# Chunk attention, soft MoE and maxout on one core: q and k repacked by token row, fp32 transposes, another order of steps and 20 ring buffers

## The chip, the cores and the metric

The kernel runs on one core of a Trainium2 chip. The metric is the device time of one execution in microseconds. Engine names are those of the profile: PE is TensorE's matmuls and PEld its weight loads, DVE is VectorE, ACT is ScalarE, POOL is GpSimd, SP is SyncE, which issues nearly all DMAs. Each engine works through its own instructions in order.

## What is computed

```python
# attention inside chunks of 64 tokens; q, k, v: 8 x 8 heads x 576 x 64
scores = scale * q_c @ k_c.T
attn = exp(scores - max(scores)); attn /= sum(attn) + 1e-9
x = (attn @ v_c) as 4608 tokens x 512
# soft MoE: 8 experts with 4 slots each, F = 1024
logits = x @ phi
d = softmax over the tokens (axis 0) of logits
slot_input = d.T @ x
slot_out[e] = maximum(slot_input[e] @ w1[e], 0) @ w2[e]
c = softmax over the slots (axis 1) of logits
x = c @ slot_out
# maxout, d_ff = 768
h = maximum(maximum(x @ m_w1, x @ m_w2), x @ m_w3)
out = h @ m_wo
```

The inputs q, k, v and phi, w1, w2 are fp32; the four maxout weights arrive as 64-bit floats, whose high and low words the kernel decodes to fp32 itself ("raw" weights below).

## The kernel before

**Loop over items.** A unit is 256 tokens; an item is half of the heads of a unit, so there are NI = 36 items. The loop at L580 walks the letters of ORDER (L63) once for each item i and calls for each its step from STEPS (L565); a step works on an item before or after i, by its offset. The order of the letters is the order of the instructions on every engine's queue, and so also of the DMA issues on SP's.

The steps that matter here: "LQ", "LK" load tile j = i + 5 of q and k (load_T: two heads of 512 tokens, 256 KB, two buffers each in raw_p); "LS" loads the last tokens of all heads in steps 1 to 4 (load_S); "LV" loads v of item i + 2 (three tiles); "LR" loads a piece of raw maxout weights (load_raw, L488); "LC" and "LD" load a quarter of an expert weight chunk (load_quarter). "VS" makes shifted copies of v on POOL (L207 to L210). "Tq", "Tk" transpose q and k on PE (emit_T), "qe", "ke" copy the result from PSUM to SBUF on ACT (emit_evac, L252). "S" makes the scores (L271), "mx" and "sub" take off the maximum on DVE, "PT" transposes the result and "PTe" takes the exponential on ACT, "PV" multiplies by v (L319), "rd", "rec", "nrm" divide by the sum on DVE, "XT" and "XTe" transpose x and copy it. Every fourth step the group steps follow: "lg" logits, "lc", "st", "ex" statistics and exponential, "eT", "eTe" its transpose, "sm", "sa" slot matmul and its sum. "df" (POOL), "da" (ACT) and "d0" (DVE) decode raw weights.

**Transposes of q and k.** emit_T reads the loaded tile as bf16 halves: for each head e of two, each token row r of four and each half h, one transpose of 128x64 by a bf16 identity, 16 for a tile; the evacuation interleaves the halves again. The tiles of "Tq", "Tk", "PT", "XT", "lg", "eT" and "sm" take turns in one PSUM pool of four tiles (ps_t). The scores have a tile of their own (ps_s), of which the columns 256 to 511 in each of two banks are unused.

**Ring buffers.** Expert weights come in 32 chunks of 1 MB. Twelve buffers are there from the start; as pools of the loop are released, open_rings adds single ones, NSLOT = 7 in all, each with its load. The expert phase begins behind the loop and a tail that finishes the last items, the last group and the slot softmax (L601 to L643). For each of eight experts emit_w1, emit_ht and emit_w2 run, and each expert's end asks for four more chunks. With expert 5 (of 0 to 7) the three loads of the output weights (load_wo) and the tiles of the combine weights take ring buffers.

**Output.** TAIL orders the entry to the maxout stage by hand; then h_mm and out_mm (L892, L929) run over blocks of 512 tokens to the end.

## Time and profile before

| what | value |
|---|---|
| median of 3 runs | 447.15 us (439.87 to 447.57) |
| the profiled execution's own time | 438.74 us |
| its span, first to last instruction | 436.9 us |
| PE busy | 401.2 us, 92% |
| DVE, ACT, POOL busy | 239.1, 214.8, 168.8 us |
| HBM read, written | 74.51 MB, 9.44 MB |

The profile is of one execution. Busy time is the time in which an engine runs instructions; matmuls overlap in the pipeline, so a merged row of matmuls can be longer than what it adds to the chain. "A <- B" is a wait of A that B's end released. The DMA share is the mean busy share of 16 DMA engines, and since transfers overlap it can pass 1. The span falls into the loop (to about 171 us), the tail of the loop and the slot softmax, the experts (from about 187 us) and the output stage (from about 241 us).

### The profile page before, as it was taken

How to read it: one execution, taken by the hardware profiler on the slowest of the kernel's cores; microseconds unless marked ns; L12 is line 12 of the kernel's file. 1: busy time of each engine (PE TensorE's matmuls, PEld its weight loads, DVE VectorE, ACT ScalarE, POOL GpSimd, SP SyncE). 2: the span in 40 equal slices, each digit the busy share in tenths (PEclk: the TensorE clock that was granted, in tenths of full speed). 3: DMA queues.
4: the chain of work that ended last, by engine and by line, in shares of the span. 5: the costliest groups of instructions: out<-in, count | busy, mean ns of one | idle time of the engine just before them, and what ended most of it. 6: DMA issues, size and time to landing. Idle time of an engine off the chain costs nothing.

```text
span 436.9 us, 13243 instructions
## 1 busy us (share of the span) xinstructions
PE 401.2 (92%) x5519; PEld 301.2 (69%) x5519; DVE 239.1 (55%) x515; ACT 214.8 (49%) x393; POOL 168.8 (39%) x291
## 2 busy tenths in 40 slices
...
PEclk9999998999999999999999799999999999999999
...
DMA packets 65275, 84.80 MB, mean 194 GB/s; under 512 B 4800, under 2 KB 42688, under 8 KB 65216
## 3 DMA queue, kind: packets, MB, share of 16 engines
...
q8 instruction: 43, 0.70, 0.7%
...
HBM read 74.51 MB, written 9.44 MB: 192 GB/s over the span
## 4 chain that ended last, share of the span: by engine, by line
PE 75%; DMA 10%; DVE 5%; ACT 4%; issue 3%; POOL 1%; SPq 1%; ACTq 0%; POOLq 0%; DVEq 0%
PE ops L929 35%; PE h L892 9%; PE pso L319 4%; DMA vt<-in_v_dram 4%; PE psqr L239 3%; PE pskr L239 3%; PE pst L354 3%; PE pss L271 3%; DMA qr<-in_q_dram 3%; PE pst L303 3%; DMA kr<-in_k_dram 2%; PE hps L706 2%; PE so L737 2%; PE slp L428 2%; PE lg L372 2%
## 5 line engine op out<-in xcount | busy, mean ns | idle before, releaser
L929 PE MATMUL ops<-wo,hhi 128*128 128x512 f32 x432 | 137.3, 399 | 0.0
L908 POOL TENSOR_TENSOR hlo<-a,hhi 128x512 fp32r<-128x512 f32 (+1 forms) x60 | 71.4, 1193 | 109.2 <-ACT hhi L905 109.2
L929 PEld LDWEIGHTS ops<-wo,hhi 128*128 128x128 f32 x432 | 81.3, 190 | 18.6
L929 PE MATMUL ops<-wo,hlo 128*128 128x512 f32 x216 | 86.0, 398 | 0.0
L901 DVE TENSOR_TENSOR a<-h,a 128x512 f32<-128x512 f32 (+1 forms) x60 | 38.2, 637 | 87.0 <-ACT a L897 86.1
L897 ACT COPY a<-h 128x512 f32<-128x512 f32 (+1 forms) x60 | 32.7, 546 | 97.1 <-PE h L892 97.0
L929 PEld LDWEIGHTS ops<-wo,hlo 128*128 128x128 f32 x216 | 41.2, 191 | 10.2
L252 ACT COPY qT<-psqr 128x1024 uint16<-128x1024 uint16 x36 | 36.7, 1020 | 19.0 <-PE pss L271 15.9
L902 DVE TENSOR_TENSOR a<-h,a 128x512 f32<-128x512 f32 (+1 forms) x60 | 38.3, 639 | 6.5 <-DVE a L901 0.5
L207 POOL COPY vt<-vt 128x256 f32<-128x256 f32 x36 | 14.6, 405 | 64.1 <-DMA vt<-in_v_dram 57.2
L905 ACT CAST hhi<-a 128x512 fp32r<-128x512 f32 (+1 forms) x60 | 34.6, 581 | 9.4 <-DVE a L902 9.4
L252 ACT COPY kT<-pskr 128x1024 uint16<-128x1024 uint16 x36 | 36.3, 1008 | 0.5 <-PE pskr L239 0.5
L287 DVE TENSOR_REDUCE mx<-pss 128x8 f32<-128x512 f32 x36 | 24.8, 688 | 20.8 <-PE pss L271 20.2
L892 PE MATMUL h<-cstt,ast 128*128 128x512 f32 (+1 forms) x120 | 32.6, 384 | 0.4 <-DVE a L902 0.3
L239 PE MATMUL psqr<-identb,qr 128*64 128x128 bf16 x512 | 22.5, 233 | 10.2 <-DMA qr<-in_q_dram 6.4
L209 POOL COPY vt<-vt 32x256 f32<-32x256 f32 x72 | 29.5, 410 | 4.3
L210 POOL COPY vt<-vt 32x256 f32<-32x256 f32 x72 | 28.9, 401 | 4.4
L359 ACT COPY xT<-pst 128x512 f32<-128x512 f32 x36 | 21.4, 593 | 17.8 <-PE lg L372 12.4
L319 PE MATMUL pso<-vt,pT 64*64 64x66 f32 x1152 | 27.1, 227 | 3.0 <-issue 2.1
L239 PE MATMUL pskr<-identb,kr 128*64 128x128 bf16 x512 | 22.1, 231 | 7.6 <-issue 3.6
L308 ACT ACTIVATE pT<-pst 128x512 f32<-128x512 f32 x36 | 21.5, 596 | 14.6 <-PE pst L303 14.5
L319 PEld LDWEIGHTS pso<-vt,pT 64*64 64x64 f32 x1152 | 21.6, 136 | 9.9 <-issue 7.8
...
## 6 DMA issues: line engine op xcount, KB each, us to landing
...
w<-in_moe_w_dram SPq DMA_DIRECT2D x44, 256.0 KB, 5.4
qr<-in_q_dram SPq DMA_DIRECT2D x32, 256.0 KB, 5.4
kr<-in_k_dram SPq DMA_DIRECT2D x32, 256.0 KB, 5.0
out_dram<-ob SPq DMA_DIRECT2D x32, 256.0 KB, 2.0
vt<-in_v_dram SPq DMA_DIRECT2D x30, 256.0 KB, 4.9
r<-in_moe_w_dram SPq DMA_DIRECT2D x18, 256.0 KB, 5.2
...
```

The source lines that it names most:

```text
L209: nc.gpsimd.tensor_copy(out=t[p:p + 32, :, 130:194], in_=t[p + 32:p + 64, :, 64:128])
L210: nc.gpsimd.tensor_copy(out=t[p + 32:p + 64, :, 64:128], in_=t[p:p + 32, :, 0:64])
L239: nc.tensor.transpose(dst, src[:, e, r, h, :], identb, tile_position=(0, 64 * e))
L252: copier(eng, j)(out=o, in_=x)
L319: nc.tensor.matmul(ps[64 * cp:64 * cp + 64, c2, 66 * h:66 * h + 66], lhsT=t[64 * c2:64 * c2 + 64, h, 64 * cp:64 * cp + 64], rhs=vt[i % NV] ...
L892: nc.tensor.matmul(p, lhsT=a_st[t][:, i, f0:f0 + 128], rhs=cst(t0, n), start=True, stop=True)
L897: nc.scalar.copy(out=h_a[b, f], in_=h_ps[b, f][0])
L901: nc.vector.tensor_tensor(out=a, in0=ps[1], in1=a, op=ALU.max)
L902: nc.vector.tensor_tensor(out=a, in0=ps[2], in1=a, op=ALU.max)
L905: nc.scalar.copy(out=h_t[b][0][:, f, :], in_=h_a[b, f])
L908: nc.gpsimd.tensor_tensor(out=h_t[b][1][:, f, :], in0=h_a.pop((b, f)), in1=h_t[b][0][:, f, :].bitcast(F32), op=ALU.subtract)
L929: nc.tensor.matmul(ps, lhsT=a[:, f, 128 * t:128 * t + 128], rhs=wo_h[f // 2][:, f % 2, w, :], start=(f == 0 and n == 0), stop=(f == FB - 1 ...
```

## The change

- A step of its own ("Rq", "Rk", emit_R) copies each loaded q or k tile into a pair tile with the token row r outermost, then head and width; q's copy runs on ACT, k's on POOL. The pair tiles have one buffer each.
- emit_T makes four fp32 transposes of 128x128 out of each pair tile, one per row r, and writes the columns into PSUM in the order in which they are used: 16 bytes apart for q, 8 bytes apart in two orders for k. The evacuation is a plain copy of 128x512 fp32.
- Transposes are emitted for tile i + 2 and not i + 3; the copy is that of tile i + 3. Probability transposes and their exponential move to the item's own step.
- Logits and the transpose of the exponential use the free columns of the scores' PSUM tile (spare).
- ORDER has the steps in another order: on SP "LD LV LR LQ LS LK LC" for "LR LC LQ LS LV LD LK"; on PE "S Tq PV sm lg eT Tk XT PT" for "S PT Tq sm eT XT PV lg Tk".
- raw-weight buffers go from three to two; NSLOT goes from 7 to 8. One ring opens at item NI - 4, one at NI - 3, and one at the start of the expert phase. To make room, the experts' hidden tiles lie in acc, which is cleared once it has been used, and the stacks of the combine weights lie in ring buffers, which are taken in another order.
- The bf16 identity goes. Other edits only rewrite views.

```diff
--- before
+++ after
@@ -61,10 +61,10 @@
         "H3 C2 X1 M2 H4 Y0 C3 o5 X2 Y1 C4 M3 H5 s1 Y2 C5 X3 Y3 M4 X4 M5 Y4 X5 Y5 s0"
     )
     ORDER = (
-        "LR qe ex S LC PT Tq LQ sm PTe mx sub sa ss da eT ke XT LS df PV LV d0 XTe "
-        "rd rec lg eTe VS LD Tk LK lc st nrm"
+        "df S LD Tq PV mx qe sm sub rd da lg eT sa LV VS Rq eTe Tk rec ke ex XT PT PTe LR "
+        "nrm lc Rk LQ LS XTe d0 LK LC st ss"
     )
-    NSLOT = 7
+    NSLOT = 8
     DUS = (0, 1, 8, 2, 3, 4, 5, 6, 7)
     J8 = 4 * DUS.index(8)
     STK = (5, 1, 2)
@@ -72,7 +72,6 @@
 
     const = ctx.enter_context(tc.tile_pool(name="const", bufs=1, side="left"))
     ident = const.tile([128, 128], F32, name="ident")
-    identb = const.tile([128, 128], BF16, name="identb")
     phi_sb = const.tile([128, KM, NS], F32, name="phi_sb")
     lsb = const.tile([128, NG, 128], F32, name="lsb")
     acc = const.tile([128, DM], F32, name="acc")
@@ -147,8 +146,9 @@
     w1_p = tc.alloc_tile_pool(name="w1p", bufs=1, side="right")
     v_p = tc.alloc_tile_pool(name="vp", bufs=1, side="right")
     q_p = tc.alloc_tile_pool(name="qp", bufs=3, side="right")
+    pair_p = tc.alloc_tile_pool(name="pair", bufs=1, side="right")
     raw_p = tc.alloc_tile_pool(name="raw", bufs=2, side="right")
-    r64_p = tc.alloc_tile_pool(name="r64", bufs=3, side="right")
+    r64_p = tc.alloc_tile_pool(name="r64", bufs=2, side="right")
     ps_t = p1.enter_context(tc.tile_pool(name="ps_t", bufs=4, space=PSUM))
     ps_q = ps_t
     ps_s = p1.enter_context(tc.tile_pool(name="ps_s", bufs=1, space=PSUM))
@@ -156,6 +156,7 @@
 
     NV = 3
     KENG, QENG, XENG = "AAAA", "AAAA", "AAAA"
+    PENG = {"qr": "A", "kr": "P"}
 
     def copier(eng, i):
         return nc.scalar.copy if eng[i % 4] == "A" else nc.vector.tensor_copy
@@ -214,42 +215,43 @@
     def last_unit(j):
         return J8 <= j < J8 + 4
 
+    pair = {}
+
+    def emit_R(j, nm):
+        if last_unit(j):
+            src = special[nm][:, 2 * (j - J8):2 * (j - J8) + 2]
+            if j == J8 + 3:
+                special.pop(nm)
+        else:
+            src = raw.pop((nm, j))
+        t = pair_p.tile([128, 4, 2, D], F32, tag=nm, name="p" + nm)
+        o = t.rearrange("p r m d -> p m r d")
+        if PENG[nm] == "A":
+            nc.scalar.copy(out=o, in_=src)
+        else:
+            (nc.vector if PENG[nm] == "D" else nc.gpsimd).tensor_copy(out=o, in_=src)
+        pair[nm, j] = t
+
     def emit_T(j, nms=("qr", "kr")):
         for nm in nms:
-            if last_unit(j):
-                src = special[nm][:, 2 * (j - J8):2 * (j - J8) + 2]
-                if j == J8 + 3:
-                    special.pop(nm)
-            else:
-                src = raw.pop((nm, j))
-            src = src.bitcast(BF16).rearrange("p m r (d h) -> p m r h d", h=2)
-            ps = ps_q.tile([128, 2, 512], BF16, tag="t", name="ps" + nm)
-            for h in range(2):
-                for r in range(4):
-                    for e in range(2):
-                        pe = ps[64 * e:64 * e + 64, h]
-                        if nm == "qr":
-                            dst = pe[:, 128 * r:128 * r + 128]
-                        else:
-                            dst = pe[:, 256 * (r // 2):256 * (r // 2) + 256]
-                            if last_unit(j):
-                                dst = dst[:, 128 * (1 - r % 2):128 * (1 - r % 2) + 128]
-                            else:
-                                dst = dst.rearrange("p (c s j) -> p c s j", s=2, j=16)[:, :, 1 - r % 2]
-                        nc.tensor.transpose(dst, src[:, e, r, h, :], identb, tile_position=(0, 64 * e))
+            src = pair.pop((nm, j))
+            ps = ps_q.tile([128, 2 * UNIT], F32, tag="t", name="ps" + nm)
+            for r in range(4):
+                if nm == "qr":
+                    if last_unit(j):
+                        o = ps.rearrange("p (c i r) -> p r i c", c=B, r=4)[:, r]
+                    else:
+                        o = ps.rearrange("p (i r) -> p r i", r=4)[:, r]
+                elif last_unit(j):
+                    o = ps.rearrange("p (c s i r) -> p s r i c", c=B, s=2, r=2)[:, 1 - r % 2, r // 2]
+                else:
+                    o = ps.rearrange("p (c s j r) -> p s r c j", s=2, j=16, r=2)[:, 1 - r % 2, r // 2]
+                nc.tensor.transpose(o, src[:, r].rearrange("p m d -> p (m d)"), ident)
             tq[nm, j] = ps
 
     def emit_evac(j, nm, eng, to):
         t = q_p.tile([128, 2 * UNIT], F32, tag=nm, name=nm)
-        n = 4 if nm[0] == "q" else 2
-        o, x = t.bitcast(U16), tq.pop((nm[0] + "r", j)).bitcast(U16)
-        if last_unit(j):
-            o = o.rearrange("p (c i r h) -> p c i r h", c=B, r=n, h=2)
-            x = x.rearrange("p h (r i c) -> p c i r h", r=n, c=B)
-        else:
-            o = o.rearrange("p (i r h) -> p i r h", r=n, h=2)
-            x = x.rearrange("p h (r i) -> p i r h", r=n)
-        copier(eng, j)(out=o, in_=x)
+        copier(eng, j)(out=t, in_=tq.pop((nm[0] + "r", j)))
         to[j] = t
 
     def emit_qevac(i):
@@ -259,6 +261,7 @@
         emit_evac(i, "kT", KENG, kT)
 
     s_ps = {}
+    spare = [None]
 
     def emit_S(i):
         ps = ps_s.tile([128, 2, 512], F32, tag="s", name="pss")
@@ -278,6 +281,7 @@
             for j in (j0, j0 + 1):
                 qT.pop(j)
                 kT.pop(j)
+        spare[0] = ps[:, :, 256:384]
         s_ps[i] = ps[:, :, 0:4 * CH].rearrange("p e (g k) -> p e g k", g=4)
 
     mxs = {}
@@ -365,8 +369,8 @@
 
     lgs = {}
 
-    def emit_logits(g):
-        lgs[g] = ps_t.tile([128, 128], F32, tag="t", name="lg")
+    def emit_logits(g, ps=None):
+        lgs[g] = ps if ps is not None else ps_t.tile([128, 128], F32, tag="t", name="lg")
         for kk in range(KM):
             for t in range(4):
                 nc.tensor.matmul(
@@ -409,8 +413,9 @@
 
     eps = {}
 
-    def emit_eT(g):
-        ps = ps_t.tile([128, 128], F32, tag="t", name="eps")
+    def emit_eT(g, ps=None):
+        if ps is None:
+            ps = ps_t.tile([128, 128], F32, tag="t", name="eps")
         nc.tensor.transpose(ps, e_sb[g], ident)
         eps[g] = ps
 
...
@@ -515,7 +519,6 @@
     sched.enter_context(tc.manual_schedule())
     if True:
         make_identity(nc, ident)
-        nc.vector.tensor_copy(out=identb, in_=ident)
         for j in range(2):
             load_T(j, "qr")
             load_T(j, "kr")
@@ -527,12 +530,15 @@
         load_raw(0)
         nc.sync.dma_start(out=phi_sb, in_=phi.rearrange("(k p) s -> p k s", p=128))
         for j in range(3):
-            emit_T(j)
-            if j < 2:
-                emit_qevac(j)
-                emit_kevac(j)
+            emit_R(j, "qr")
+            emit_R(j, "kr")
             load_T(j + 2, "qr")
             load_T(j + 2, "kr")
+            if j == 2:
+                break
+            emit_T(j)
+            emit_qevac(j)
+            emit_kevac(j)
         load_raw(1)
         nc.gpsimd.memset(ones1, 1.0)
 
@@ -565,16 +571,17 @@
         STEPS = {
             "LR": lambda i: load_raw(i + 1) if 0 < i < len(dec) - 1 else None,
             "LQ": item(lambda j: load_T(j, "qr"), 5), "LK": item(lambda j: load_T(j, "kr"), 5),
+            "Rq": item(lambda j: emit_R(j, "qr"), 3), "Rk": item(lambda j: emit_R(j, "kr"), 3),
             "LV": item(load_v, 2), "LC": lstep_c, "LD": lambda i: lstep_c(i) if i % 2 else None,
             "LS": lambda i: load_S(i - 1) if 1 <= i <= 4 else None,
             "VS": item(emit_vswap, 0),
-            "qe": item(emit_qevac, 2), "S": item(emit_S, 0), "PT": item(emit_PT, -1), "PTe": item(emit_PTe, -1),
+            "qe": item(emit_qevac, 2), "S": item(emit_S, 0), "PT": item(emit_PT, 0), "PTe": item(emit_PTe, 0),
             "da": dstep("a"), "df": dstep("f"), "ke": item(emit_kevac, 2), "ex": group(emit_exps, 7), "sm": group(emit_slot_mm, 9),
-            "sa": group(emit_slot_acc, 9), "Tq": item(lambda i: emit_T(i, ("qr",)), 3), "mx": item(emit_max, 0),
+            "sa": group(emit_slot_acc, 9), "Tq": item(lambda i: emit_T(i, ("qr",)), 2), "mx": item(emit_max, 0),
             "sub": item(emit_sub, 0), "XT": item(emit_XT, -2), "XTe": item(emit_XTe, -2),
             "d0": dstep("m"), "PV": item(emit_PV, -1), "rd": item(emit_rd, -1),
-            "rec": item(emit_rec, -1), "nrm": item(emit_norm, -1), "eT": group(emit_eT, 8), "eTe": group(emit_eTe, 8),
-            "Tk": item(lambda i: emit_T(i, ("kr",)), 3), "lg": group(emit_logits, 6), "lc": group(emit_lcopy, 6),
+            "rec": item(emit_rec, -1), "nrm": item(emit_norm, -1), "eT": group(lambda g: emit_eT(g, spare[0][:, 1]), 8), "eTe": group(emit_eTe, 8),
+            "Tk": item(lambda i: emit_T(i, ("kr",)), 2), "lg": group(lambda g: emit_logits(g, spare[0][:, 0]), 6), "lc": group(emit_lcopy, 6),
             "st": group(emit_stats, 6), "ss": group(emit_ssum, 7),
         }
         for i in range(NI):
@@ -582,13 +589,15 @@
                 STEPS[name](i)
             if i == len(dec) + 1:
                 r64_p.release()
-                open_rings(1)
                 nc.vector.tensor_reduce(
                     out=sel, in_=ident.rearrange("p (g s) -> p s g", g=4), axis=AX.X, op=ALU.max
                 )
             if i == NI - 4:
                 raw_p.release()
                 open_rings(1)
+            if i == NI - 3:
+                pair_p.release()
+                open_rings(1)
         q_p.release()
         open_rings(1)
 
@@ -599,8 +608,6 @@
                 nc.tensor.transpose(warm[:, 0:128], ident, ident)
 
         last = NG - 1
-        emit_PT(NI - 1)
-        emit_PTe(NI - 1)
         emit_eT(last - 1)
         emit_eTe(last - 1)
         emit_XT(NI - 2)
@@ -649,7 +656,8 @@
     ps2a = tc.alloc_tile_pool(name="ps2a", bufs=1, space=PSUM, reuse_waits="tile")
     ps2b = tc.alloc_tile_pool(name="ps2b", bufs=2, space=PSUM, reuse_waits="tile")
     same = m_p.tile([128, 4, NS], F32, name="same")
-    hzb = [m_p.tile([128, KF, NS], F32, name=f"hz{i}") for i in range(2)]
+    hzb = [acc.rearrange("p (b k s) -> p b k s", b=2, k=KF)[:, i] for i in range(2)]
+    open_rings(1)
     ctok = lsb.rearrange("p g (t s) -> p (g t) s", t=4)
     wo_raw = []
 
@@ -682,8 +690,6 @@
         nc.vector.tensor_tensor(out=ct, in0=ct, in1=cm.to_broadcast([128, n, NS]), op=ALU.mult)
 
     if True:
-        for t in hzb:
-            nc.gpsimd.memset(t, 0.0)
         for g in range(4):
             nc.vector.tensor_copy(out=same[:, g, :], in_=sel)
         sip = ps2.tile([128, KM, NS], F32, tag="b", name="sip")
@@ -691,6 +697,7 @@
             nc.tensor.matmul(
                 sip[:, kk, :], lhsT=acc[:, 128 * kk:128 * kk + 128], rhs=dg, start=True, stop=True
             )
+        nc.gpsimd.memset(acc, 0.0)
         siT = m_p.tile([128, KM, NS], F32, name="siT")
         nc.vector.tensor_copy(out=siT, in_=sip)
         tot = ps2.tile([128, 1], F32, tag="b", name="tot")
...
@@ -818,10 +826,13 @@
             if e < 3:
                 emit_c(e)
             if e == 5:
+                cst_t.append(rings[0].tile([128, 2048], F32R, tag="w", name="cstt"))
+                ahl_t0.append(rings[0].tile([128, 2048], F32R, tag="w", name="ahl"))
                 for _ in range(FB // 2):
                     load_wo()
-                for o, w in CT:
-                    cst_t.append(rings[0].tile([128, 2048], F32R, tag="w", name="cstt"))
+                for _ in range(2):
+                    cst_t.insert(-1, rings[0].tile([128, 2048], F32R, tag="w", name="cstt"))
+                stk.extend(t[:, 1536:2048] for t in (cst_t[2], ahl_t0[0]))
                 a_st.append(cst_t[2][:, 768:768 + 3 * TW].rearrange("p (i n) -> p i n", i=3))
                 next_stack(1)
             if e == 6:
...
```

## Rows read from the trace of the kernel before

**Rows 1.** Table by stretch: busy us of each engine, clock, DMA share, GB/s.

```profile
33.30:61.40 28.10, 25.39 (x702) 19.70 (x698) 18.82 (x43) 20.54 (x33) 15.31 (x36) 1.00 0.91 265
61.40:100.50 39.10, 35.28 (x918) 27.03 (x914) 26.84 (x65) 27.75 (x49) 21.95 (x53) 0.96 1.03 339
...
137.60:171.50 33.90, 31.73 (x854) 23.94 (x850) 25.18 (x60) 24.12 (x42) 15.22 (x38) 1.00 0.89 292
```

**Rows 2.** Timeline of PE, start and us: first and last of 36 scores.

```profile
11.33 0.69 PE L271 MATMUL pss<-kT,qT 64*64 64x64 f32 x32
...
171.55 0.69 PE L271 MATMUL pss<-kT,qT 64*64 64x64 f32 x32
```

**Rows 3.** Chain of waits, start and us: one step, then group steps.

```profile
33.41 0.62 PE pss L271 x32
34.03 0.59 PE pst L303 x4
34.62 0.57 PE psqr L239 x16
35.19 0.59 PE pst L354 x4
35.77 0.63 PE pso L319 x32
...
40.22 1.01 PE lg L372 x32
...
74.84 1.04 PE slp L428 x8
```

**Rows 4.** Who waited for whom, PE: us in total, times, longest.

```profile
PE psqr L239 <- DMA qr<-in_q_dram: 6.4, 4, 4.0
...
PE pskr L239 <- DMA kr<-in_k_dram: 3.4, 4, 2.4
...
PE psqr L239 <- ACT kT L252: 1.9, 1, 1.9
```

**Rows 5.** Timeline of PE: first and last of eight gaps by issue.

```profile
44.59 0.41 PE L239 MATMUL psqr<-identb,qrs 128*64 128x128 bf16 x7 [1.19 <-issue]
...
170.15 0.46 PE L319 MATMUL pso<-vt,pT 64*64 64x66 f32 x16 [0.38 <-issue]
```

**Rows 6.** Page: busy us, instructions; the instruction queue's packets, MB, share.

```profile
PE 401.2 (92%) x5519; PEld 301.2 (69%) x5519; DVE 239.1 (55%) x515; ACT 214.8 (49%) x393; POOL 168.8 (39%) x291
...
q8 instruction: 43, 0.70, 0.7%
```

**Rows 7.** Page: granted TensorE clock in 40 slices of 10.9 us.

```profile
PEclk9999998999999999999999799999999999999999
```

**Rows 8.** Single lines, ns minimum/median/maximum: bf16 and fp32 transposes.

```profile
L239 PE MATMUL psqr<-identb,qr x512: 216/219/316, 4.0 to 161.8; 128*64 128x128 bf16 x171
...
L303 PE MATMUL pst<-ident,sx x144: 269/273/329, 14.3 to 175.6; 128*128 128x128 f32 x144
```

**Rows 9.** Groups by line, busy us and mean ns: copies.

```profile
L252 ACT COPY qT<-psqr 128x1024 uint16<-128x1024 uint16 x36 | 36.7, 1020 | 19.0 <-PE pss L271 15.9 <-PE psqr L239 3.1
...
L359 ACT COPY xT<-pst 128x512 f32<-128x512 f32 x36 | 21.4, 593 | 17.8 <-PE lg L372 12.4 <-PE pst L354 5.2
...
L905 ACT CAST hhi<-a 128x512 fp32r<-128x512 f32 x48 | 29.9, 624 | 8.5 <-DVE a L902 8.5
...
L207 POOL COPY vt<-vt 128x256 f32<-128x256 f32 x36 | 14.6, 405 | 64.1 <-DMA vt<-in_v_dram 57.2 <-PE pso L319 3.3 <-PE pst L303 1.5
```

**Rows 10.** The same view, DVE: the subtraction of the maximum.

```profile
L292 DVE TENSOR_TENSOR sx<-pss,mx 128x512 f32<-128x512 f32 x36 | 24.9, 692 | 3.7
```

**Rows 11.** Page: DMA issues of raw weights, KB, us to landing.

```profile
r<-in_moe_w_dram SPq DMA_DIRECT2D x18, 256.0 KB, 5.2
```

**Rows 12.** Timeline of PE: x transposes behind the last scores.

```profile
173.94 0.63 PE L354 MATMUL pst<-ident,x 128*128 128x128 f32 x4 [1.10 <-DVE x L339]
```

**Rows 13.** Expert weight tiles, matmuls' wait for landing: us, times.

```profile
  DMA w<-in_moe_w_dram: 0.6, 2
```

18 lines of the change are left out of this document (9 added, 9 removed).

## The prediction

> **What bounds the kernel now.** I read the table of stages first, then the starts of the score matmuls, then the chain of waits, then single lines. The table of stages cuts the span where the work changes. Up to about 171 us the 36 items of the attention loop run; then come the end of the slot softmax and the expert matmuls; from 241 us on the output matmuls keep TensorE without a gap. The change touches the loop and the entry to the experts. In the loop two resources are nearly full at the same time [rows 1]: between 61.4 and 100.5 us the DMA share is 1.03 and PE is busy 35.28 of 39.10 us; before that the share is 0.91, after it 0.89. So a gain on one of the two is cut off by the other.
>
> The first score matmul starts at 11.33 us and the last at 171.55 us [rows 2]: 35 steps in 160.2 us, 4.58 us each. The chain of waits shows one step in which PE never stops [rows 3]: scores 0.62, probability transposes 0.59, q transposes 0.57, x transposes 0.59, PV 0.63, and the k transposes, the same work as q's, 0.57: together 3.57 us. Every fourth step adds the logits (1.01) and the slot matmuls (1.04 as the merged piece shows it), 0.51 us a step on average. The floor of PE is thus 4.08 us, and 0.50 us a step, 17.4 us in the loop, is something else. [...] PE waits for q and k to land: 6.4 and 3.4 us, of which 4.0 us is the very first load [rows 4], so 5.8 us. PE has gaps in the middle of a row of matmuls that the profile puts down to "issue" [rows 5]: in the loop after 30 us there are eight longer than 0.3 us, the first 1.19 and the last 0.38, 6.16 us in all. They stand in the middle of a tile, where no semaphore is due. The instruction queue moved 43 packets, and 5519 weight loads and 5519 matmuls [rows 6] make 257 PE instructions a packet; gaps of this kind look like a packet that came late while the data queue was full. [...]
>
> **The change part by part.** *Transposes on PE.* For each of q and k, 16 bf16 transposes give way to 4 fp32 ones of 128x128. The x and probability transposes are four of that size and take 0.59 us, the sixteen take 0.57 us [rows 3]: +0.02 us, twice a step, 36 tiles each: +1.4 us. The new ones write their columns 8 or 16 bytes apart in PSUM; no matmul of before does that, so this is open. Bounds: nothing, or a stream at half the rate. [...]
>
> [...]
>
> *Instructions.* A step loses 24 matmuls and 24 weight loads, 48 PE instructions of some 229 a step (64 scores, 64 PV, 64 q and k, 16 other transposes, about 21 for the group steps): 21 in 100. If late packets scale with the packets, the 6.16 us of gaps lose 1.3 us. Bounds 0 and -6.2.
>
> *Copies.* The two evacuations become plain 128x512 copies: from 1.02 us to the 0.593 us of the x copy, twice [rows 9]. ACT gets the q copy, 0.62 us by its 128x512 copy between SBUF tiles (the cast of h), POOL the k copy, 0.81 us as two of its 128x256 copies. ACT loses 0.23 us a step. POOL's five small copies of 0.4 us [rows 9] and one decode make about 2.5 us a step, so 3.3 us of 4.58: still free, but k's copy stands behind them in POOL's queue. What ACT's shorter work is worth is bounded by the one wait of PE for a k evacuation, 1.9 us [rows 4], and by nothing; I take -1.0.
>
> *Where a late load is felt.* Before, a late q or k stops PE in the transposes. Now it stops ACT or POOL one step earlier, and the transposes come a step after the copy. From k's copy near the end of a step to its transposes in the next are some 2 us in which PE goes on. Of the 5.8 us this can save all or, if ACT's or POOL's queue only hands the wait on, nothing. Behind q's copy on ACT stand k's evacuation, the exponential and the x copy, for which PE waits; behind k's copy on POOL the next decode and the next v swap, which PV needs. I take -1.5.
>
> *Order.* Logits and the e transpose leave the ring of four PSUM tiles for spare columns of the scores' tile. The next scores then wait for their evacuations (DVE, ACT); these end within the step, before the scores are due, so I cost it at nothing; if DVE ran late, the next scores would wait for one small copy, in one step of four. The probability transposes move up to their own step; what they wait for, the maximum and the subtraction (0.69 us each [rows 10], the maximum being about as long), passes under q transposes, PV, k transposes and x transposes (2.4 us). On SyncE the weight load LR moves from the head of a step to behind the v load and, with two buffers for three, must wait for the decode on DVE that empties its buffer, in the second half of the step. Behind LR stand q, the special loads, k and a quarter of weights. Cost: a raw load then has about one step and a little, 5 us, to its use on POOL and ACT; it needs 5.2 us [rows 11]. POOL can absorb one to two us. I take nothing; the bound is in the rivals.
>
> *Entry.* The copies put ACT and POOL ahead of the first transposes. ACT's chain copy, evacuate, evacuate, copy, evacuate, evacuate from the landing of q, 4.0 us after the start [rows 4], gives the first scores at about 11.5 us: +0.2. *End of the loop.* The last probability transposes now precede the post-loop work, and the 1.10 us wait of an x transpose for DVE [rows 12] may go: bounds 0 and -1.1, I take -0.8. *Twentieth ring buffer.* One more megabyte is under way when the experts begin; PE waits for expert weights 0.6 us in all [rows 13], so 0 to -0.6: -0.3. Tiles moved into accumulator and ring, one memset put after another matmul, cost nothing: they lie under the expert matmuls.
>
> Sum: +1.4 - 1.3 - 1.0 - 1.5 - 0.8 - 0.3 + 0.2 = -3.3 us. The profiled execution took 438.74 us (span 436.9 and 1.8 around it), so 435.4 us. The median shown is 447.15, with one run at 439.87: the profiled execution stands with the lower one. The forecast is in its terms.
>
> **The rivals.** *Faster by more than 2%: both resources fill.* If the later transposes take every wait for data out of the loop, the DMA share rises to the 1.03 of the middle. 33.3 to 61.4 us then shrinks by 28.1 x 0.12 / 1.03 = 3.3 us; the start, 22 us, if its share is like that row's, by 2.6; 137.6 to 171.5 us has eight steps of 4.24 us and can only fall to PE's 4.08, 1.3; the half-clock stretch gives 1.5 (an estimate: two tenths of a slice of 10.9 us, less what DMA holds back). These 8.7 us stand for the two middle terms (-2.5); with the others (-0.8) the gain is 9.5: 429.2 us. For it: the lower shares. Against: early loads are slow to issue and are small, which the change leaves.
>
> *Slower: the strided PSUM write.* [...] It decides from about (8.8 + 3.3) / 288 = 42 ns a transpose. For it: strides that no row has. [...]
>
> *Slower: the raw load starves the queue.* If LR on SyncE holds back q and k each step until DVE has decoded, and a step waits 0.4 us more (an estimate: the raw load then lands 1.5 to 2 us too late and POOL absorbs the larger part), 30 steps with decode cost 12 us: 447.4 us. It decides when the raw load needs over about 7 us instead of 5.2. Against: where the queue is full there is work enough behind it.
>
> **How the numbers follow.** Two per cent (8.8 us) is about what a measurement of this kernel can tell from no change. The forecast, a small gain within 2%: 0.46. Both resources fill: 0.30. Strided write: 0.15. Starved queue: 0.09. So faster 0.30, same 0.46, slower 0.24. The range runs from 427, a little under the first rival, to 450, up to the strided rival: it leaves out about 0.1 at either end. The forecast's own range is 430 to 442.
>
> **What would show it.** In the profile after: four q transposes in 0.59 us and not 0.8 or more; evacuations of 0.59; the k copy on POOL near 0.8; a step of the loop near 4.5 us and first scores at 11.5; fewer instruction packets (36 of 43) and fewer "issue" gaps; no long wait of POOL for raw weights; output stage unchanged. Wrong would be: longer transposes, a longer step with DMA share under 0.9 in the middle, or a loop shorter by 9 us.

## The result, and the profile after

The changed kernel takes 429.40 us (median of 4 runs, 427.06 to 431.45); the kernel before took 444.88 beside it (median of 4, 439.87 to 447.57). The ratio is 0.9709, 95% interval [0.9647, 0.9771]: 2.9% faster; it is taken over the runs in the faster of two states, and so lies nearer to 1 than that of the medians (0.965). The prediction said 435.4 us and "within 2%". The time lies in its range, and on the number of its first rival (429.2), but not by the road that this rival took. Both numbers were counted from the profiled execution of before, 438.74 us, which lies 6.1 us under the median: the forecast was a gain of 3.3 us, the rival's 9.5, and the medians differ by 15.5. That they come so close to 429.40 is in part luck.

The profiled executions took 438.74 us (before) and 431.45 us (after), so between the profiles only 7.3 us are to be found. Three pieces hold them all. The columns are from the timeline of PE, in us: start of the first scores (first S), start of the last, the loop between them, and start of the first expert matmul ("hps").

| profiled execution | first S | last S | loop | us a step | last S to experts | experts |
|---|---|---|---|---|---|---|
| before | 11.33 | 171.55 | 160.22 | 4.58 | 15.83 | 187.38 |
| after | 10.40 | 166.08 | 155.68 | 4.45 | 13.95 | 180.03 |
| difference | -0.93 | | -4.54 | | -1.88 | -7.35 |

From the experts on the two run nearly alike: 7.35 us apart there, 7.6 at the end of the span (436.9 and 429.3).

Within the loop the whole difference stands in the first five steps: from the first to the sixth scores before takes 22.00 us and after 17.45 (sixth scores at 33.34 and 27.85 us); the other thirty steps take 138.22 and 138.22. In these five steps before has a gap by issue and a wait for k; after has neither, only a wait of 0.7 us for k's copy. Timeline of PE, before:

```profile
22.91 0.64 PE L239 MATMUL pskr<-identb,kr 128*64 128x128 bf16 x15 [2.58 <-issue]
...
32.77 0.64 PE L239 MATMUL pskr<-identb,kr 128*64 128x128 bf16 x16 [2.36 <-DMA kr<-in_k_dram]
```

So this pair of profiles shows no gain behind the fifth step. Three near twins of after (e4, e5 and e17 below) take 135.5, 135.4 and 133.9 us for the thirty steps, 2.7 to 4.3 less than before.

Timeline of PE, after, the first half of the first scores and the last scores (start and us), which answer to [rows 2]:

```profile
10.40 0.71 PE L274 MATMUL pss<-kT,qT 64*64 64x64 f32 x16
...
166.08 0.69 PE L274 MATMUL pss<-kT,qT 64*64 64x64 f32 x32
```

Table by stretch, after, with the columns of [rows 1]; the last line is the whole loop:

```profile
28.00:59.00 31.00, 27.88 (x569) 22.36 (x569) 20.14 (x48) 20.89 (x43) 21.68 (x45) 0.89 0.91 264
59.00:99.00 40.00, 33.74 (x731) 26.06 (x726) 26.56 (x65) 25.87 (x57) 27.33 (x62) 0.96 0.99 324
99.00:133.00 34.00, 30.98 (x719) 24.60 (x716) 26.65 (x63) 26.01 (x56) 25.07 (x56) 1.00 1.05 352
133.00:166.00 33.00, 30.97 (x719) 24.48 (x717) 25.99 (x62) 22.99 (x49) 22.22 (x51) 1.00 1.00 337
...
10.40:166.08 155.68, 140.48 (x3073) 111.68 (x3072) 111.17 (x261) 107.96 (x226) 109.06 (x240) 0.97 0.98 315
```

The same view of before, over its loop:

```profile
11.33:171.55 160.22, 142.53 (x3855) 109.66 (x3851) 110.83 (x256) 114.31 (x191) 80.57 (x193) 0.99 0.95 302
```

The DMA share of the last stretch of the loop was 0.89 [rows 1] and is 1.00; that of the whole loop went from 0.95 to 0.98. Length times share is 152 us in both (160.22 x 0.95, 155.68 x 0.98): the transfers of the loop are the same work, and at the highest share seen, 1.05, this work would still take 145 us (an estimate). Between 28 and 59 us the share is 0.91, as it was in before [rows 1]. PE idled 17.7 us in the loop (160.22 - 142.53) and idles 15.2 now.

Chain against chain, this is one of the shortest steps of after; [rows 3] has the shortest of before. Timeline of PE, start and us; the distance between two starts is what a group costs:

```profile
98.83 0.69 PE L274 MATMUL pss<-kT,qT 64*64 64x64 f32 x32
99.46 0.66 PE L249 MATMUL psqr<-ident,pqr 128*128 128x128 f32 x4
100.04 0.70 PE L323 MATMUL pso<-vt,pT 64*64 64x66 f32 x32
100.67 0.66 PE L249 MATMUL pskr<-ident,pkr 128*128 128x128 f32 x4
101.16 0.60 PE L358 MATMUL pst<-ident,x 128*128 128x128 f32 x4
101.60 0.60 PE L307 MATMUL pst<-ident,sx 128*128 128x128 f32 x4
102.13 0.29 PE L274 MATMUL pss<-kT,qT 64*64 64x64 f32 x4
```

3.30 us from scores to scores, where before needed 3.57. The q transposes, between scores and PV, cost 0.58, as any group of four did before. But k, x and probability transposes stand in one row and cost 0.49, 0.44 and 0.53: 0.28 us less than three times 0.58. That is the whole difference of the two steps, and no term of the forecast had it. It is a floor and not the usual step: behind its first five steps before comes down to it once (its next shortest step is 3.80 us), after five times.

Who waited for whom, PE in the loop of after (us in total, times, longest):

```profile
PE pss L419 <- DVE sx L296: 2.2, 6, 0.7
PE psqr L249 <- ACT pqr L230: 2.2, 1, 2.2
PE pss L376 <- DVE sx L296: 2.1, 5, 0.7
PE pss L274 <- ACT kT L254: 1.9, 2, 1.7
...
PE pso L323 <- issue: 1.5, 2, 1.3
PE pss L274 <- issue: 1.3, 1, 1.3
```

Waits by "issue" come to 3.0 us in the loop (0.2 of them before the logits); the same view of before's loop has 9.1 us of them (3.6 and 3.0 in k and q transposes, 2.1 in PV, 0.4 in x transposes), the gaps of [rows 5] with those ahead of 30 us. No wait for a DMA is left on PE in the loop; the other waits, 8.3 us of which 4.3 were for loads, are now 12.0 us, for DVE, ACT and POOL.

Groups by line, after: the new copies and the evacuations, for [rows 9] (busy us, mean ns of one, idle time before them):

```profile
L254 ACT COPY qT<-psqr 128x512 f32<-128x512 f32 x36 | 21.2, 588 | 8.8 <-PE psqr L249 7.3
L254 ACT COPY kT<-pskr 128x512 f32<-128x512 f32 x36 | 21.1, 585 | 13.0 <-PE pskr L249 12.6
...
L232 POOL COPY pkr<-kr 128x512 f32<-128x512 f32 x32 | 20.0, 624 | 14.1 <-DMA kr<-in_k_dram 5.8 <-issue 2.3 <-PE pskr L249 2.0
L230 ACT COPY pqr<-qr 128x512 f32<-128x512 f32 x32 | 19.7, 616 | 3.9 <-DMA qr<-in_q_dram 3.9
```

### The profile page after: what moved, and what is told of

The parts are those of the page before. It is cut to its first block, busy times and chain, and to the rows that moved or that the text cites. A ratio compares the mean times of both kernels' runs of the same rounds, so it can differ in the third digit from the quotient of the medians.

```text
span 429.3 us, 11618 instructions
## 1 busy us (share of the span) xinstructions
PE 396.6 (92%) x4655; PEld 300.7 (70%) x4655; DVE 237.8 (55%) x514; ACT 206.7 (48%) x429; POOL 193.0 (45%) x326
## 4 chain that ended last, share of the span: by engine, by line
PE 73%; DVE 11%; DMA 9%; ACT 3%; issue 2%; POOL 1%; SPq 0%; ACTq 0%; POOLq 0%; DVEq 0%
PE ops L940 36%; PE h L903 9%; DMA qr<-in_q_dram 4%; PE pss L274 4%; PE pskr L249 3%; DMA r<-in_moe_w_dram 3%; PE pso L323 3%; PE psqr L249 2%; PE hps L713 2%; PE pst L358 2%; DVE sx L296 2%; PE pss L376 2%; DVE mx L291 2%; PE pst L307 2%; PE so L744 2%
## 5 line engine op out<-in xcount | busy, mean ns | idle before, releaser
L249 PE MATMUL psqr<-ident,pqr 128*128 128x128 f32 x144 | 25.4, 303 | 8.1 <-ACT pqr L230 8.1
L274 PE MATMUL pss<-kT,qT 64*64 64x64 f32 x1152 | 27.5, 230 | 5.2 <-ACT kT L254 1.9
L211 POOL COPY vt<-vt 32x256 f32<-32x256 f32 x72 | 30.0, 417 | 4.4
L323 PE MATMUL pso<-vt,pT 64*64 64x66 f32 x1152 | 29.1, 230 | 2.5 <-issue 1.5
L210 POOL COPY vt<-vt 32x256 f32<-32x256 f32 x72 | 29.4, 408 | 4.3
L274 PEld LDWEIGHTS pss<-kT,qT 64*64 64x64 f32 x1152 | 21.6, 138 | 12.5 <-issue 5.4
L323 PEld LDWEIGHTS pso<-vt,pT 64*64 64x64 f32 x1152 | 23.0, 138 | 9.8 <-issue 5.1
L885 POOL TENSOR_TENSOR wo<-tmp,wo 128x512 fp32r<-128x512 f32 x6 | 8.2, 1368 | 47.8 <-ACT wo L882 47.5
L254 ACT COPY kT<-pskr 128x512 f32<-128x512 f32 x36 | 21.1, 585 | 13.0 <-PE pskr L249 12.6
L903 PEld LDWEIGHTS h<-cstt,ast 128*128 128x128 f32 x120 | 22.7, 198 | 6.3 <-DVE a L913 0.6
```

The lines of the kernel that those rows point to most:

```text
L211: nc.gpsimd.tensor_copy(out=t[p + 32:p + 64, :, 64:128], in_=t[p:p + 32, :, 0:64])
L249: nc.tensor.transpose(o, src[:, r].rearrange("p m d -> p (m d)"), ident)
L274: nc.tensor.matmul(ps[64 * cp:64 * cp + 64, e, 128 * a + 64 * c2:128 * a + 64 * c2 + 64], lhsT=qT[j0 + a][64 * e:64 * e + 64, c0:c0 + CH], ...
L323: nc.tensor.matmul(ps[64 * cp:64 * cp + 64, c2, 66 * h:66 * h + 66], lhsT=t[64 * c2:64 * c2 + 64, h, 64 * cp:64 * cp + 64], rhs=vt[i % NV] ...
L903: nc.tensor.matmul(p, lhsT=a_st[t][:, i, f0:f0 + 128], rhs=cst(t0, n), start=True, stop=True)
```

## The experiments

Ratios are to runs of the kernel before beside each (their medians are 441.86 to 445.45 us), with a 95% interval; the last columns are from the profiled execution: the shortest step that has all six groups, behind the first five steps; us a step from the first scores to the last; the gaps of PE by "issue" of 0.25 us or more between 30 and 176 us, in us; and the matmuls of PE, each with a weight load.

| kernel | us, median | ratio | shortest step | us a step | issue gaps | PE matmuls |
|---|---|---|---|---|---|---|
| before | 444.88 | 1 | 3.56 | 4.58 | 6.2 | 5519 |
| after | 429.40 | 0.9709 [0.9647, 0.9771] | 3.30 | 4.45 | 2.6 | 4655 |
| e1_bf16 | 443.97 | 1.0101 [1.0049, 1.0153] | 3.41 | 4.79 | 12.1 | 5519 |
| e2_bfp32 | 436.63 | 0.9893 [0.9785, 1.0001] | 3.31 | 4.45 | 6.6 | 4655 |
| e7_split | 440.25 | 0.9959 [0.9915, 1.0004] | 3.91 | 4.73 | 0 | 4655 |
| e13_bxt | 441.55 | 1.0001 [0.9946, 1.0056] | 3.41 | 4.67 | 7.2 | 5519 |
| e4_19 | 428.55 | 0.9716 [0.9610, 0.9822] | 3.30 | 4.39 | 3.0 | 4655 |
| e5_ring | 429.94 | 0.9755 [0.9640, 0.9871] | 3.30 | 4.35 | 3.0 | 4655 |
| e17_19_ring | 428.91 | 0.9630 [0.9569, 0.9691] | 3.30 | 4.33 | 3.8 | 4655 |
| e12_dec | 430.81 | 0.9776 [0.9698, 0.9853] | 3.30 | 4.53 | 1.6 | 4655 |
| e14_rows | 435.29 | 0.9869 [0.9789, 0.9948] | 3.39 | 4.53 | 3.0 | 4655 |
| e15_rows_ring | 433.60 | 0.9815 [0.9746, 0.9884] | 3.39 | 4.51 | 3.3 | 4655 |
| e16_pt_first | 443.40 | 0.9990 [0.9940, 1.0040] | 4.18 | 4.74 | 3.4 | 4655 |

**The transposes back to bf16, the new order kept.** Sixteen bf16 transposes straight from the loaded tile as before, no copies, three raw buffers; order, offsets, logits' place and 20 ring buffers as after.

```diff
-            src = pair.pop((nm, j))
-            ps = ps_q.tile([128, 2 * UNIT], F32, tag="t", name="ps" + nm)
-            for r in range(4):
...
-                nc.tensor.transpose(o, src[:, r].rearrange("p m d -> p (m d)"), ident)
+            src = src.bitcast(BF16).rearrange("p m r (d h) -> p m r h d", h=2)
+            ps = ps_q.tile([128, 2, 512], BF16, tag="t", name="ps" + nm)
...
+                        nc.tensor.transpose(dst, src[:, e, r, h, :], identb, tile_position=(0, 64 * e))
...
-        copier(eng, j)(out=t, in_=tq.pop((nm[0] + "r", j)))
+        copier(eng, j)(out=o, in_=x)
```

> The changed kernel with one part undone: q and k go through the 16 bf16 transposes again, straight from the loaded tiles (three buffers each in the place of the pair tiles), with the old evacuation; the order of steps, the logits' place and the 20 buffers stay. Theory A (the gain is PE's: four kinds of 128x128 fp32 transposes, three of them in one row, where a group of four takes 0.44 us instead of 0.59, and fewer instructions): the shortest step rises from 3.30 to about 3.45 us, the gaps put down to issue return to about 6 us, time 434 to 437 us. Theory B (the gain is the order and the later transposes, which still hold here): 428 to 431 us.

443.97 us, 1% slower than before and beyond both expectations: without the fp32 transposes the new order is a small loss. The shortest step is 3.41 us, and the issue gaps double against before; of the 12.0 us by which the loop is longer than after's, they make 9.5. Timeline of PE, e1_bf16, one of its ten gaps; the bracket is the idle time ahead:

```profile
82.66 0.36 PE L240 MATMUL psqr<-lsb,qr 128*64 128x128 bf16 x6 [1.70 <-issue]
```

Its first scores start at 8.78 us, though, 1.6 us ahead of after's: so much do the copies cost at the entry, net of the shorter evacuations.

**The fp32 transposes in the old order.** Before's order, offset of three tiles and 19 ring buffers, with the pair copies and the four transposes; the raw load of a step is issued one step later, since it has two buffers.

```diff
+    PENG = {"qr": "A", "kr": "P"}
...
-        "LR qe ex S LC PT Tq LQ sm PTe mx sub sa ss da eT ke XT LS df PV LV d0 XTe "
+        "LR Rq qe ex S LC PT Tq LQ sm PTe mx sub sa ss da eT ke XT LS Rk df PV LV d0 XTe "
...
-            "LR": lambda i: load_raw(i + 1) if 0 < i < len(dec) - 1 else None,
+            "LR": lambda i: load_raw(i) if 1 < i < len(dec) else None,
```

> The kernel before in its old order, with the pair copies (of tile i + 3, in the same step ahead of the transposes) and the four fp32 transposes; two raw-weight buffers, 19 ring buffers. With the run of bf16 transposes in the new order this completes a table of two by two. Theory A (kinds of matmul and number of instructions): like the changed kernel, PE changes its kind four times a step, the shortest step is about 3.3 us and gaps put down to issue are under 4 us: 429 to 434 us. Theory B (it is the new order that lets the transposes be used): within 2% of before, 436 to 445 us.

436.63 us; the interval just reaches 1. The step is the first theory's, the time the second's. Its loop is as short as after's, 4.45 us a step, and its shortest step 3.31: in the old order "PT Tq XT" is a row of three as soon as Tq is of the same kind as its neighbours. What it lacks against after lies outside the loop: the first scores start at 14.11 us, 3.7 us later, because with the old offset a third tile is copied and transposed ahead of them; and from the last scores to the experts it needs 17.27 us, 3.3 more. Of these, 1.62 us are a gap by issue in the middle of the last scores, behind which the granted clock from 172 to 176 us was 0.60: they need not belong to the order. So in these two profiles the fp32 transposes made the loop shorter, and the new order pays at the entry, by transposing two tiles ahead and not three. In the times the new order alone gives 1.010, the fp32 transposes alone 0.989 and both 0.971: neither does it alone. Of one pair of profiles the size is only rough: the loops of after, e4, e5 and e17, near the same kernel, run from 151.6 to 155.7 us.

**Same instructions, more changes between kinds.** After, with scores and PV cut into two halves and a group of transposes put between the halves.

```diff
-        "df S LD Tq PV mx qe sm sub rd da lg eT sa LV VS Rq eTe Tk rec ke ex XT PT PTe LR "
+        "df S LD Tq S2 Tk PV XT P2 mx qe sm sub rd da lg eT sa LV VS Rq eTe rec ke ex PT PTe LR "
```

> The changed kernel with the same instructions on every engine, but scores and PV cut into halves that stand between the transposes on PE (half scores, q transposes, half scores, k transposes, half PV, x transposes, half PV, probability transposes). Theory A (rows of equal transposes are what is cheap): each group of four takes 0.55 to 0.59 us again, the shortest step rises from 3.30 to about 3.55 us, the loop by 5 to 8 us, time 434 to 437 us. Theory B (the gain is in loads and waits): 428 to 431 us.

440.25 us, slower than either theory expected: nearly the whole gain is gone, with not one instruction more on PE. Timeline of PE, e7_split:

```profile
103.23 0.46 PE L278 MATMUL pss<-kT,qT 64*64 64x64 f32 x16
103.62 0.66 PE L249 MATMUL psqr<-ident,pqr 128*128 128x128 f32 x4
104.20 0.46 PE L278 MATMUL pss<-kT,qT 64*64 64x64 f32 x16
104.60 0.66 PE L249 MATMUL pskr<-ident,pkr 128*128 128x128 f32 x4
105.18 0.46 PE L333 MATMUL pso<-vt,pT 64*64 64x66 f32 x16
105.58 0.66 PE L371 MATMUL pst<-ident,x 128*128 128x128 f32 x4
...
106.56 0.66 PE L313 MATMUL pst<-ident,sx 128*128 128x128 f32 x4
107.14 0.34 PE L278 MATMUL pss<-kT,qT 64*64 64x64 f32 x8
```

Every transpose group is back at 0.58, and a half of scores or PV costs 0.40, not half of 0.63. The step takes 3.91 us with eight changes of kind; after takes 3.30 with four: 0.61 / 4 = 0.15 us for each change. In the sum that is 35 x 0.61 = 21 us, of which 11 come out in the time (440.25 - 429.40). The run has none of after's 2.6 us of gaps by issue; that a slower PE covers other waits too is likely, but wasn't traced.

**One row of two, in the kernel before.** The x transposes directly behind the probability transposes; bf16 transposes stay.

```diff
-        "LR qe ex S LC PT Tq LQ sm PTe mx sub sa ss da eT ke XT LS df PV LV d0 XTe "
+        "LR qe ex S LC PT XT Tq LQ sm PTe mx sub sa ss da eT ke LS df PV LV d0 XTe "
```

> The kernel before with one letter moved: x transposes stand directly behind the probability transposes on PE. Theory A: the two fp32 groups together take 0.14 us less a step (0.44 and 0.58 for twice 0.59), the shortest step falls from 3.57 to about 3.43 us, and the time by 2 to 5 us. Theory B: no change within 2 us.

No gain: 441.55 us, ratio 1.0001. The row does its part: the shortest step falls from 3.56 to 3.41 us, 0.15 us for one change less with the same instructions. Two waits take a part of it back. Who waited for whom, PE, e13_bxt:

```profile
PE pss L271 <- issue: 5.0, 3, 2.4
...
PE pst L354 <- DVE x L339: 3.1, 6, 1.0
```

The x transposes now come before DVE has made x (3.1 us, 1.9 in before), and the issue gaps are 7.2 us where before had 6.2. Together that is 2.2 us of the 5.3 that 35 steps could give (35 x 0.15); the rest isn't shown.

**Other parts taken back.** 19 ring buffers (e4_19); logits and the e transpose in the ring of four PSUM tiles (e5_ring; of the two long lines only the changed entries are shown); both (e17_19_ring).

```diff
-    NSLOT = 8
+    NSLOT = 7
...
-    open_rings(1)
     ctok = lsb.rearrange("p g (t s) -> p (g t) s", t=4)
```

> The changed kernel with 19 ring buffers and not 20. Theory: PE hardly waits for expert weights, so no more than 1 us slower, 429 to 431 us; if the last weights or the output weights come to be what ends, the experts' phase (33.9 us) grows by up to the 2.5 us of a megabyte: 432 us.

```diff
-"eT": group(lambda g: emit_eT(g, spare[0][:, 1]), 8)
-"lg": group(lambda g: emit_logits(g, spare[0][:, 0]), 6)
+"eT": group(emit_eT, 8)
+"lg": group(emit_logits, 6)
```

> The changed kernel with one part undone: logits and the transpose of the exponential take a tile of the ring of four again, and not the free columns of the scores' tile. In the changed kernel these two wait for the subtraction on DVE that reads the same tile, about 5 us each over the run. If that wait is on the path: 425 to 428 us. If the ring of four then holds PE back for evacuations as much: 429 to 432 us. If the free columns are worth what they were made for: over 432 us.

> The changed kernel with two of its parts taken back at once: 19 ring buffers, and logits and the transpose of the exponential in the ring of four PSUM tiles. If neither is worth anything, alone or together, 427 to 431 us, the same as the changed kernel. If each carried some of the gain and the singles were luck, 432 us or more.

428.55, 429.94 and 428.91 us: all three agree with the changed kernel's time. The 20th buffer and the new place of the logits are worth nothing that can be measured, alone or together. e17 has no wait of the logits for DVE (4.3 us in after) and a step of 4.33 us; the 4 us that this is shorter in one profile don't show in the medians.

**Later decode.** The decode on POOL and ACT waits for the raw loads: in after, POOL waited 19.3 us for raw weights to land (12.2 in before) and ACT 16.7. Here both decode steps come later in the step.

```diff
-        "df S LD Tq PV mx qe sm sub rd da lg eT sa LV VS Rq eTe Tk rec ke ex XT PT PTe LR "
+        "S LD Tq PV mx qe sm sub rd lg eT sa LV VS df Rq eTe Tk rec ke da ex XT PT PTe LR "
```

> The changed kernel with the decode of raw weights moved back in the step: POOL's part behind the v swap, ACT's part behind the k evacuation. Theory C (with two buffers the raw load comes late; POOL and ACT wait for it 19 and 17 us in all and hold back v swap, q copy and evacuations): those waits fall under 10 us each, the steps behind 27.8 and 122.6 us shorten, time 424 to 427 us. Theory D (the DMA queue is full anyway, the wait only shows at another place): 428 to 431 us.

POOL's wait falls to 0.9 us and the time stays: 430.81 us. The wait only moved, as the second theory had it: POOL now waits 20.4 us for v (4.2 in after), ACT 28.4 us for q (3.0), and the decode on DVE 24.4 us for ACT, in 17 waits. The DMA share of the stretches from 59, 99 and 133 us is 1.03, 1.03 and 0.98.

**Is an issue gap a packet that queues behind data?** Before, without the quarter loads of expert weights; the chunks of the first ring buffers are loaded all together at the end of the 32nd step.

```diff
     def lstep_c(i):
...
-            if i > 4:
-                load_quarter()
+            return
...
+            if i == len(dec) + 1:
+                while ring_n[0] < NRING:
+                    load_chunk()
```

> The kernel before with the expert weights of the first ring buffers loaded behind the step in which the raw weights end, and not in quarters inside the loop; so in most of the loop the DMA queue has less to do, and the whole gets longer at its end by up to 25 us. Theory E (gaps put down to issue are instruction packets that come late behind data): gaps in the loop fall from about 9 to under 3 us and the middle of the loop runs faster, the last scores before 168 us. Theory F (the gaps belong to PE itself): the gaps stay at 6 to 10 us.

458.16 us as a whole (one run), as the weights now come late; what counts is the loop. Table by stretch, e8_noq, to be held against [rows 1]:

```profile
61.40:100.50 39.10, 35.47 (x935) 27.13 (x934) 28.23 (x68) 28.93 (x53) 23.66 (x55) 1.00 0.81 255
```

With the DMA share at 0.81 in place of 1.03 there are still 5.3 us of gaps of 0.25 us or more from 30 us on, none over 1.11; neither theory had that number. So a gap does not need a full data queue, against what the prediction supposed; in runs with more on the queue single ones reach 1.9 and 2.4 us (e1, e13). The loop itself is 152.72 us, 7.5 less than before's and 3.0 less than after's, with before's six changes a step: the last scores start at 164.09 us. In these two profiles the quarter loads thus cost before's loop 7.5 us, more than the 4.5 that the change gave it.

Where the gaps stand does point to the instruction stream. Some of them, with the start of the matmul behind each and the number of PE matmuls ahead of it, counted in the traces:

```
kernel   start, us   matmuls ahead   since the one before
before       98.56         2122
            114.38         2503   381 = 3 x 127
            134.63         3011   508 = 4 x 127
            139.92         3138   127
            150.81         3391   253 = 2 x 126.5
e1_bf16      99.99         2119
            115.52         2500   381 = 3 x 127
            121.02         2627   127
            126.54         2754   127
            131.70         2880   126
after        90.19         1478
            125.86         2235   757 = 6 x 126.2
```

127 matmuls with 127 weight loads are 254 PE instructions, close to the 257 a packet that the prediction counts from [rows 6]; after has 2 x 4655 of them to 37 packets, 252 each. That the gaps are waits for a packet is argued from these counts and not shown. The places come back in other kernels of the same count: 2122 matmuls stand ahead of a gap in e8 too, 2235 in e12. Some of these places have a gap of about a microsecond, others none: in before, from 44.59 to 93.22 us, 1139 matmuls (9 x 126.6) pass without a gap inside a tile. The ten kernels here with 4655 matmuls have 3.0 us of gaps by issue in that stretch on average (0 to 6.6), the four with 5519 have 7.7 (5.3 to 12.1). In e12, e14, e15 and e16 the larger part of these gaps stands ahead of a tile's first matmul and not inside a tile, so it need not be of this kind (e14 below); inside a tile the ten have 2.2 us on average.

**Two kinds a step.** After, with PV directly behind the scores and all four transpose groups behind it (e14_rows), then with the logits in the ring of four (e15_rows_ring), then with the probability transposes ahead of the x transposes and the decode later (e16_pt_first).

```diff
-        "df S LD Tq PV mx qe sm sub rd da lg eT sa LV VS Rq eTe Tk rec ke ex XT PT PTe LR "
+        "df S LD PV Tq mx qe sm sub rd da lg eT sa LV VS Rq eTe Tk rec ke ex XT PT PTe LR "
```

> The changed kernel with PV moved ahead of the q transposes, so that PE has scores and PV next to each other and then q, k, x and probability transposes in one row: PE changes between 64-wide products and 128x128 transposes twice a step instead of four times. Theory K (a change of kind costs about 0.15 us): the shortest step falls from 3.30 to about 3.0 us; since the DMA share is already 1.0 to 1.04 from 59 us on, little of the 36 x 0.3 = 10.8 us comes out: 424 to 429 us. Rival: PV now starts straight behind the scores and has to wait for the exponential of the step before (ACT) or for the shifted v, and takes the gain back: shortest step 3.2 or more, 429 to 433 us with new waits of PE for ACT.

> e14_rows with logits and the transpose of the exponential back in the ring of four PSUM tiles. In the changed kernel PE waited 2.1 us before the logits and 2.2 us before that transpose for DVE to read the scores, since they share its tile. If these waits lie on the path now that PE's step is shorter, 1 to 4 us faster than e14_rows; if DMA sets the step, the same as e14_rows within 1 us.

435.29 and 433.60 us, slower than after by 1 to 1.5%: the rival was right in its cause, and even its 433 us were too few for e14. The 1.7 us between the two runs lie within their spread. The row of four costs 1.89 us where after pays 0.58 + 1.46, but PV comes too early. Timeline of PE, e14_rows:

```profile
98.86 0.69 PE L274 MATMUL pss<-kT,qT 64*64 64x64 f32 x32
99.72 0.70 PE L323 MATMUL pso<-vt,pT 64*64 64x66 f32 x32 [0.17 <-issue]
100.35 0.66 PE L249 MATMUL psqr<-ident,pqr 128*128 128x128 f32 x4
100.84 0.60 PE L249 MATMUL pskr<-ident,pkr 128*128 128x128 f32 x4
101.28 0.60 PE L358 MATMUL pst<-ident,x 128*128 128x128 f32 x4
101.71 0.60 PE L307 MATMUL pst<-ident,sx 128*128 128x128 f32 x4
102.24 0.46 PE L274 MATMUL pss<-kT,qT 64*64 64x64 f32 x16
```

Timeline of ACT, e14_rows, the exponential:

```profile
99.02 0.60 ACT L312 ACTIVATE pT<-pst 128x512 f32<-128x512 f32 x1 [0.35 <-PE pst L307]
```

The exponential runs to 99.62, and PV, which reads it, starts 0.86 us after the scores instead of the 0.52 that it needs in e16, where it doesn't wait. The profile puts this wait down to "issue"; ACT's row shows what it is. The 0.86 us stand in most steps. In others PV waited for the shifted v (6.2 us in 12 waits on POOL), which is also due earlier now. Without that wait, 0.35 us, the step would be 3.04 (an estimate).

```diff
-        "df S LD Tq PV mx qe sm sub rd da lg eT sa LV VS Rq eTe Tk rec ke ex XT PT PTe LR "
+        "S LD PV Tq mx qe sm sub rd lg eT sa LV VS df Rq eTe Tk PT PTe rec ke da ex XT LR "
```

> e15_rows_ring with the probability transposes and their exponential ahead of the x transposes, and the weight decode behind the v swap on POOL. In e14_rows the exponential ended at 99.62 us and PV began at 99.72, 0.17 us after the scores had ended: PV waited for ACT. Here the exponential comes one group of transposes (0.44 us) earlier. Theory K (each change of kind costs about 0.15 us, and only that wait hid it): the shortest step falls from 3.38 to 3.1 to 3.2 us, with PV directly behind the scores, and the time is 425 to 430 us. Rival (the passage from scores to PV has a price of its own): PV still starts over 0.8 us after the scores' start, the shortest step stays at 3.3 or more, and the time at 431 to 435 us.

443.40 us, a miss of both expectations, in time and in the shortest step (4.18 us). PV does follow directly, 0.52 us behind the start of the scores, so scores to PV shows no price of its own. But the probability transposes now wait for DVE. Timeline of PE, e16_pt_first:

```profile
100.17 0.69 PE L274 MATMUL pss<-kT,qT 64*64 64x64 f32 x32
100.69 0.65 PE L323 MATMUL pso<-vt,pT 64*64 64x66 f32 x32
...
104.25 0.63 PE L307 MATMUL pst<-ident,sx 128*128 128x128 f32 x4 [1.89 <-DVE rd L333]
```

Timeline of DVE, e16_pt_first, the same time:

```profile
101.40 0.45 DVE L514 SCALAR_TENSOR_TENSOR wm<-wm,r 128x256 int32<-128x256 int32 x1 [1.79 <-issue]
...
102.69 0.68 DVE L291 TENSOR_REDUCE mx<-pss 128x8 f32<-128x512 f32 x1
103.41 0.69 DVE L296 TENSOR_TENSOR sx<-pss,mx 128x512 f32<-128x512 f32 x1
```

The decode on ACT was moved behind the k evacuation and runs from 100.86 to 101.31 us; DVE's decode, which reads it, starts at 101.40, and the group statistics and the maximum stood behind that. The subtraction ended at 104.10 and PE, which reads it, started at 104.25 after a wait of 1.89 us, though the profile names the next DVE instruction. Such waits come to 12.6 us, 12 of them. The run mixed two edits, the earlier transposes and the later decode, and which of the two did it wasn't separated.

## Why the prediction was right in time and wrong in its sum

**Transposes, +1.4 us: the step that failed.** It took the 0.59 us of a group of four [rows 3] for the price of the transposes, wherever they stand. The price is that of the transposes plus that of passing between the 64-wide products and the 128x128 transposes. Shortest steps by changes of kind in a step: eight 3.91 (e7), six 3.56 (before), five 3.41 (e1, e13), four 3.30 to 3.31 (after, e2, e4, e5), two 3.04 (e14, less its wait). Where the instructions are the same a change comes to 0.13 to 0.15 us: e7 against after 0.15, before against e13 0.15, after against e14 0.13. The kinds are scores and PV (tiles of 64x64), bf16 transposes (128x64) and fp32 transposes (128x128): in a step of before they change six times, with four equal fp32 groups four times. The forecast's instruction count was right and its sign was not: -0.26 us a step, not +0.04, or -9.1 us over 35 steps if all of it came out. It did not all come out: in the pair of profiles the steps behind the fifth gained nothing. That the changes weigh in the time is shown by e7, 11 us for four more of them with the same instructions. What was overlooked is that the price of a group depends on its neighbours; the counts of changes and the steps here agree with that. The trace of before had a row for it, behind the loop, where probability transposes meet another 128x128 transpose (timeline of PE, before):

```profile
175.24 0.66 PE L303 MATMUL pst<-ident,sx 128*128 128x128 f32 x4
175.73 0.27 PE L414 MATMUL eps<-ident,et 128*128 128x128 f32 x1
```

0.49 us to the next start, with four transposes of the same size, where the same group costs 0.59 in [rows 3].

**Strided PSUM: right.** The forecast's sum has no term for the strides. The transposes that write 16 and 8 bytes apart have the same median as the contiguous ones of [rows 8], 273 ns (single lines, after):

```profile
L249 PE MATMUL psqr<-ident,pqr x144: 272/273/475, 4.8 to 158.5; 128*128 128x128 f32 x144
...
L249 PE MATMUL pskr<-ident,pkr x144: 272/273/476, 6.2 to 160.7; 128*128 128x128 f32 x144
```

The ends of matmuls are modelled in the profile, so starts are the better witness: in e14's row the k transposes, 8 bytes apart, take 0.44 us to the next start, and so do the contiguous x transposes in after. The rival needed 42 ns for each transpose. The upper end of the prediction's range, 450 us, rests on an added time for each transpose that no run shows: the strided transposes took the same 273 ns as the contiguous ones.

**Instructions, -1.3 us: too small.** 37 packets came, where 36 were forecast; but the time of the gaps does not go with the packets. Waits of PE by issue fell from 9.1 to 3.0 us in the loop, and e1, with before's count, has 12.1 between 30 and 176 us alone. From before to after, a fifth fewer instructions in the loop came with less than half of the gaps. Why some of the places have a gap and others none stays open: e8 shows that a full data queue is not needed, and e7, with a slower PE, has none at all.

**Where the rest went.** The two gains are worth 9.1 + 6.1 us in sum; the loop got 4.5 in the profile, all of it in the first five steps. PE's other waits grew from 8.3 to 12.0 us, and the mean granted clock of the loop fell from 0.99 to 0.97: between 30 and 38 us it was 0.57, behind a wait in which ACT stood 3.45 us for a raw load and then copied a late q. Timeline of ACT, after:

```profile
29.10 0.54 ACT L500 ACTIVATE wm<-r 128x384 f32<-128x384 f32 x1 [3.45 <-DMA r<-in_moe_w_dram]
30.07 0.62 ACT L230 COPY pqr<-qr 128x512 f32<-128x512 f32 x1 [0.42 <-DMA qr<-in_q_dram]
```

Timeline of PE, after, what waited for that copy:

```profile
30.74 1.11 PE L249 MATMUL psqr<-ident,pqr 128*128 128x128 f32 x4 [2.20 <-ACT pqr L230]
```

This is the forecast's "ACT's queue only hands the wait on". Of its -1.5 us for late loads the rows give about that much: PE waited 4.3 us for loads in the loop of before, and 2.9 us for the two copies in that of after (2.2 for q's, 0.7 for k's); but the low clock stands right behind the longest of these waits. The -1.0 us for k's evacuation did not come: PE still waits 1.9 us for it, now ahead of the scores. Behind 59 us the DMA share is 0.99 to 1.05, and there the other resource seems to cut what PE gains: e5, e12 and e17 each take a wait away and none is faster. But of the first rival's four terms the two largest, 3.3 and 2.6 us, asked for a share of 1.03 ahead of 61 us, and it stayed at 0.89 to 0.91; the clock's 1.5, an estimate from [rows 7], went the other way: the half-clock stretch of before had a granted clock of 0.58, 0.50, 0.50 and 0.71 in the four microseconds from 69 us, after had 0.57 in the eight from 30 us. The start did get 4.5 us shorter, but by the wait and the gap that went and not by a higher share. That its 429.2 us were hit is luck. The prediction also passed over a row when it read the share behind 100.5 us as 0.89: from 100.50 to 137.60 us it was 0.99 in before, so there was little left to fill.

**Smaller terms.** Evacuations of 0.588 and 0.585 us and a q copy of 0.616 came as forecast, k's copy at 0.624 and not 0.81. Logits beside the scores were costed at nothing: PE waits 4.3 us for DVE there, and nothing is lost by it (e5). The 20th ring, -0.3: nothing (e4). The entry, +0.2: -0.93. The forecast let the scores wait for the last of its chain, the second tile's k evacuation, which runs from 10.51 to 11.10 us; their first half starts ahead of it, at 10.40, and only the second half behind it, at 11.15. The end of the loop, -0.8: -1.88; the 1.10 us wait of [rows 12] is gone, another went from 0.53 to 0.27, and one group of probability transposes (0.49) no longer stands there. POOL does wait longer for raw weights, 19.3 us for 12.2, against the sign that the forecast gave; but e12, which takes this wait away, is no faster, so the starved queue did not cost its 12 us.

**Not settled.** PE's busy time in the loop fell only from 142.5 to 140.5 us; 2% less clock accounts for some 3 of the missing 7 us (an estimate, 0.02 x 155.7), the rest was not traced. And against typical runs of before the gain is 13 to 15 us, against its profiled one 7.3: the profiles show half of it, and where the other half lies is open.
